# Attention and MLP in one kernel: v moved to partitions 32 to 95, its neighbour rows copied on chip, the halves swapped, and a new written order

## The chip, the cores and the metric

The kernel runs on one core of one Trainium2 chip. The metric is device time in microseconds (us). The core has five engines that work side by side, each through its own queue and in its own order: TensorE (PE in the profile: matrix products; PEld is its weight load), VectorE (DVE), ScalarE (ACT), GpSimd (POOL), which here mostly issues the loads, and SyncE (SP), which issues the stores. Sixteen DMA engines move the data between HBM and SBUF.

## The reference, cut to what matters

```python
B, H, S, D = 4, 8, 768, 64;  block, window = 32, 16
k_sum = k.reshape(B, H, S//32, 32, D).max(axis=3)      # 24 block maxima of k per head
v_sum = v.reshape(B, H, S//32, 32, D).mean(axis=3)     # 24 block means of v per head
scores_l = q @ k.T / 8, kept only where |i - j| < 16   # a band of 31 keys
scores_s = q @ k_sum.T / 8 + log(32)                   # 24 coarse keys
a = softmax(concat([scores_l, scores_s]))
x = (a @ concat([v, v_sum])) as [3072, 512]            # heads side by side
h = x @ w_in;  g = h * clip(h + 3, 0, 6) / 6;  out = g @ w_out    # w_in 512x2048, w_out 2048x512
```

All inputs and the output are float32 in HBM. The kernel loads with a conversion to bf16.

## The kernel before, in words

**Tiling of the attention.** A batch has 768 query rows per head, cut into NQ = 12 tiles of 64 queries (QB). With a band of 31 keys a tile needs a window of 96 key rows (WIN), and the 24 block maxima stand beside them, so that the product for one tile and one head has 120 keys (KEYS). `kaug[p]` holds k transposed for the pair p of heads, tile by tile: columns 0 to 63 are the tile's own rows, 64 to 95 the 32 rows of the next tile, 96 to 119 the maxima. A tile t therefore covers keys 64t to 64t+95 and queries 64t+16 to 64t+79; the last tile wraps round to the first rows, and its mask differs. `vaug[b % 2]` holds v in the same layout with the keys on partitions: rows 0 to 63 are loaded, rows 64 to 95 are those of the next tile, rows 96 to 119 are the block sums, and a column of ones (32 for the block rows) next to the 64 columns of v gives the softmax denominator. Each tile takes 66 columns (VW) per head.

**How each batch is loaded.** Batch 0 loads k and half of q in natural layout (`load_k`, `load_q`) and transposes on PE (`k_step`, `q_step`). Batches 1 to 3 load k and q by `load_raw` into `kraw` and `qraw` and transpose 32x32 blocks on VectorE (`turn`, lines 588 and 592); q is written in 16-row halves there, eight DMAs of 16 partitions a batch (line 375), k in four DMAs of 32 partitions (line 367). v comes by `load_v`, four DMAs of 64 partitions (line 385). Its 32 neighbour rows are copied on chip for batch 0 (`halo`) and loaded from HBM a second time for the other batches (`load_vhalo`, line 393, and a small SP DMA, line 395). `vsum_first` and `vsum` form the block sums by products with the indicator `ind` and spread them to 12 tiles a head.

**The stages.** `scores` (line 519, exp on ACT at 527, mask on DVE at 531), `values` and `finish` (products at 632, division at 663 and 667, transposes at 682) give x for half a batch: three tiles T of 128 rows. Half 0 is tiles t = 0 to 5 and half 1 tiles 6 to 11. The MLP takes x by half batches s = 0 to 7: `f1` (line 700: four products of 384 columns for one of 16 blocks ft; then ACT at 705 and DVE at 707 make g) and `f2` (line 720: 16 accumulating products of 512 columns for 128 rows, copied at 432 and stored at 730).

**What sets the order.** Every step is an operation with a key such as `F20.0`: the letter is the stage (K, Q, V, H loads; I, O weights; k, q, w transposes; s scores; u sums; h halo; v values; F, G the two MLP products), then batch or half batch and index, then the step's number in it. The string `ORDER` (lines 29 to 82) lists all keys once; each engine runs its operations in the order in which they stand there, and a suffix `:A` or `:D` says that ACT or DVE takes a copy. Nothing is reordered at run time: an instruction that waits holds all that is behind it on its engine. Costs and `dma=` figures in the code are what the writer of the order assumed; no time here is taken from them. Before 22 us, `keep` (line 803) puts products of constants into PE's waits.

So the first MLP product of half batch 0 is F00.0, the first of batch 1 is F20.0; w1p.0 and w1p.1 are the k and q transposes of batch 1, pair p; s1p0.0 are its scores; Q001 and Q011 are the second half of q of batch 0.

Of the kernel before, what the change touches and what calls it, by code (L numbers as in the profile page):

```python
# [15 lines left out]
D = 64  # L16
BLK = 32
# [4 lines left out]
VW = 66  # L22
# [19 lines left out]
F10.3 F12.1 F10.2 F12.2 F10.6 F10.4 F10.9 F10.5 F10.7 F10.8 F11.0 F10.10 F10.11 F11.6 F11.1 F11.9 F11.2 F11.7 F11.8 F11.10
F11.11 F12.6 F12.7 F12.8 F12.9 F12.10 F12.11 w12.0 G01.1 F13.0 F13.1 w13.0 F13.2 w11.0 w13.3 w10.0 w12.3 G01.2 G01.3 F12.3
F13.9 G01.4:A G02.0 G02.1 G02.2 G02.3 F11.3 F13.10 w11.2:A F12.4 F12.5 G02.4:A w12.2:A F13.3 F11.4 F13.4 w10.2:A w13.2:A
w12.4 w11.3 w11.4 w11.1 w11.5:D G00.0 G00.1 s110.0 s110.1 s110.3 w12.1 w13.1 w12.5:D w13.5:A G00.2 G00.3 s120.0 s120.1
s120.3 w13.4 w10.1 F13.5 w10.3 F11.5 w10.4 w10.5:D F13.11 V10.0 V13.0 V11.0 V23.0 V12.0 H1.0 K20.0 K22.0 V20.0 K21.0 Q231.0
K23.0 Q220.0 V22.0 V21.0 Q200.0 Q221.0 Q201.0 Q211.0 Q210.0 Q230.0 s130.0 G00.4:A F13.6 G12.0 s130.3 s130.1 F13.7 G00.5
G01.5 H1.1 G02.5 s120.2 s110.2 s130.2 s100.0 s100.1 F13.8 s100.2 s110.4 s100.3 G12.1 u1.0 u1.1:A u1.3:A u1.5:A G12.2 G12.3
G12.4:A u1.4:D u1.2:D v10.0 s120.4 v10.1 v10.5 v10.6 v10.2 s100.4 u1.7:A u1.6:A u1.9:A G11.0 G11.1 v12.0 v10.3 v10.4:A
u1.8:A v12.1 v12.2 s130.4 G11.2 v10.7 v12.3 v10.8:D G11.3 v12.4:A v13.0 F20.0 F20.3 G11.4:A F20.1 F20.4 v13.5 v13.1 v13.2  # L50
v13.6 F20.9 v13.3 v15.0 F20.10 F20.2 F20.5 F20.11 v15.1 v15.2 F20.6 F21.0 F20.7 F20.8 F21.1 V30.0 V31.0 V32.0 V33.0 F21.2
w21.0 F21.6 G10.0 F21.7 v13.4:A F21.8 F21.3 v15.3 v13.7 F21.9 F22.3 F21.4 F21.5 w20.0 F22.0 G10.1 F21.10 F22.4 v15.4:A
F21.11 F22.1 F22.5 F22.9 F23.0 F22.2 w20.3 F22.10 F22.11 F23.1 w21.2:A v13.8:A F23.2 w22.0 F22.6 u2.0 F22.7 F22.8 w21.3
G10.2 F30.0 F23.6 G10.3 w22.2:A F30.1 w20.4 F30.2 F30.3 F23.3 G10.4:A w22.3 w22.4 G22.0 G22.1 w20.1 u2.1:A w20.2:A F23.7
F23.4 w20.5:A F30.4 G12.5 u2.3 u2.5 G11.5 u2.4 u2.2 F23.5 F23.8 w22.1 s200.0 s200.1 s200.3 F30.5 w22.5:A F31.6 F23.9 G22.2
w23.1 F23.10 F31.7 s220.0 F23.11 F31.8 w21.4 w21.1 w21.5:D F30.9 G22.3 F31.0 F31.3 s220.3 s220.1 s210.0 G22.4:A H2.0 Q301.0
Q330.0 w23.0 K32.0 Q311.0 H3.0 F31.1 w23.5:A Q310.0 Q300.0 Q320.0 Q331.0 F31.2 F31.4 s200.4 F30.10 F30.11 F31.5 G20.0 G20.1
F30.6 F32.3 F33.0 Q321.0 K33.0 K31.0 K30.0 s210.1 s210.3 w23.3 F30.7 w23.4 s200.2 F30.8 w23.2:A F32.4 F33.1 u3.0 u3.1:D
s220.2 F33.2 s220.4 s210.2 G20.2 s230.0 s230.1 s230.3 s230.2 F32.5 G20.3 F31.9 F32.9 F31.10 F31.11 G20.4:A H2.1 G10.5 u3.3
u3.5 H3.1 G20.5 G22.5 v20.0 v20.1 v20.5 v20.2 v20.6 F33.9 G32.0 F32.10 F33.10 v22.0 F33.3 v20.3 F33.11 F32.0 G32.1 F33.4  # L60
v20.4:A v20.7 F32.1 v20.8:A v22.1 v22.2 F33.5 s230.4 F32.2 s210.4 v22.3 F32.11 v22.4:A F33.6 F32.6 F33.7 F32.7 v23.0 F33.8
v23.1 F32.8 F40.0 F40.1 F41.3 G32.2 F40.9 G32.3 F40.10 F41.4 v23.2 F40.2 F40.11 F41.5 v23.5 v23.6 F42.3 F41.9 F42.4 F42.5
F43.0 v25.0 F41.10 G32.4:A v23.3 F41.11 F42.0 F40.6 G30.0 G30.1 v23.4:A F43.1 F42.1 F40.7 v25.1 w30.1 F42.2 F43.2 F40.8
F41.0 F41.1 F41.2 v25.2 F40.3 F40.4 w30.5:A w33.1 w32.1 F42.6 G30.2 G30.3 F42.9 G30.4:A F42.7 v23.7 v23.8:A F42.10 G21.0
G21.1 G21.2 F40.5 w31.0 F42.8 F42.11 F43.3 F43.4 w30.0 w30.3 F43.6 w30.4 F43.5 w31.3 G21.3 F43.7 w32.5:D G21.4:A G21.5 v25.3
# [784 lines left out]
```

## Time and profile before

| | |
|---|---|
| median of three runs | 231.94 us (231.37 to 234.25) |
| the profiled execution's own time | 233.64 us |
| its span, first to last instruction | 231.9 us |
| bytes read from HBM, written | 29.60 MB, 6.29 MB |
| POOL's load queue | 117280 packets, 14.81 MB written to SBUF |
| first F00 product, first F20 product, last product's end | 30.30 us, 79.81 us, 227.29 us |

The busy time of an engine is the union of its instructions. Mean durations of single instructions include their latency, so that the sum of the means is somewhat more than the busy time. A wait is given as "engine and line <- engine and line that released it". In the table of windows each engine has its busy time and, in brackets, its instructions; then come the granted TensorE clock (1.00 is full), the DMA engines' busy share, and the rate in GB/s of the bytes on the written side, which are bf16 for loads.

### The profile page before, as it was taken

Reading aid. Unit: us, or ns where it says so; the run is one execution under the profiler, and the core shown is the slowest. Engines: PE = TensorE matmul, PEld = TensorE weight load, DVE = VectorE, ACT = ScalarE, POOL = GpSimd, SP = SyncE. Lnnn points to the kernel's source line nnn. Section 1 sums busy time; section 2 is a strip of 40 time slices with the busy share of each in tenths; the row PEclk is TensorE's granted clock in tenths of the full one; section 3 lists DMA queues with packets and bytes.
Section 4 is the critical chain, followed back from the end, with each engine's and each line's share of the span. In section 5 each row is a group of like instructions: output and inputs, shape, how many; then the busy total and the mean of one; then the engine's idle time right before and its main releaser. Section 6 shows DMA issues by size and latency. Waiting matters only on the chain.

```text
span 231.9 us, 5321 instructions
## 1 busy us (share of the span) xinstructions
PE 217.3 (94%) x2175; PEld 121.8 (52%) x2175; DVE 156.7 (68%) x327; ACT 126.5 (55%) x258; POOL 72.8 (31%) x86
## 2 busy tenths in 40 slices
PE   7899699999989997989999889999999999999991
PEld 2365476555445563545565445555555555555560
DVE  2489689789897669889785499945955645454201
ACT  2287567774588854768654535675552543434101
POOL 7994481357754734707741200000000000000000
PEclk9999979999999999999999999999999999999998
DMA  5999999999999999999999990132002030012013
GB/s 76 169 123 182 191 206 196 119 77 87 95 120 176 186 103 86 85 114 146 84 142 89 127 71 0 45 80 84 3 11 85 0 136 3 0 45 90 3 68 114
DMA packets 126585, 22.14 MB, mean 95 GB/s; under 512 B 116960, under 2 KB 123616, under 8 KB 126560
## 3 DMA queue, kind: packets, MB, share of 16 engines
q0 software_dynamic: 117280, 14.81, 217.7%
q1 hardware_dynamic: 9280, 6.98, 12.7%
q8 instruction: 17, 0.28, 0.7%
q14 instruction: 8, 0.07, 0.1%
HBM read 29.60 MB, written 6.29 MB: 155 GB/s over the span
## 4 chain that ended last, share of the span: by engine, by line
PE 58%; DMA 18%; issue 9%; POOL 9%; ACT 2%; DVE 2%; DVEq 0%; POOLq 0%
PE h L700 26%; PE o L720 22%; DMA kraw<-in_k_dram 13%; DMA qnat<-in_q_dram 5%; PE h L720 4%; POOL vaug L385 3%; ACT at L527 2%; PE S L519 1%; PE S L632 1%; POOL qraw L375 1%; POOL qnat L357 1%; PE S L682 1%; POOL knat L346 1%; POOL win L417 1%; POOL kraw L367 1%
## 5 line engine op out<-in xcount | busy, mean ns | idle before, releaser
L700 PE MATMUL h<-x,win 128*128 128x384 bf16 (+1 forms) x536 | 95.0, 321 | 3.1 <-DVE g L707 3.1
L705 ACT ACTIVATE r<-h 128x384 f32<-128x384 f32 x128 | 60.4, 493 | 59.4 <-PE h L700 58.7
L707 DVE SCALAR_TENSOR_TENSOR g<-r,h 128x384 bf16<-128x384 f32 x128 | 67.5, 545 | 33.9 <-ACT r L705 32.1
L720 PE MATMUL o<-wout,g 128*128 128x512 bf16 x336 | 82.3, 379 | 0.2 <-ACT ot L432 0.2
L700 PEld LDWEIGHTS <-win 128*128 128x128 bf16 x536 | 49.9, 99 | 37.5 <-issue 3.6
L720 PEld LDWEIGHTS <-g 128*128 128x128 bf16 x400 | 38.1, 98 | 36.3
L375 POOL DMA_DIRECT2D qraw<-in_q_dram x24 | 21.3, 890 | 29.1 <-issue 10.5
L527 ACT ACTIVATE at<-S 120x768 bf16<-120x768 f32 x32 | 24.8, 812 | 7.1 <-PE S L519 7.1
L367 POOL DMA_DIRECT2D kraw<-in_k_dram x12 | 15.8, 1317 | 13.5 <-issue 12.0
L385 POOL DMA_DIRECT2D vaug<-in_v_dram x16 | 15.1, 949 | 4.8 <-PE h L700 3.1
L592 DVE STREAM_TRANSPOSE qaug<-qraw 128x800 bf16<-128x800 bf16 x12 | 11.8, 998 | 6.2 <-DMA kraw<-in_k_dram 3.3
L667 DVE TENSOR_TENSOR xn<-S,rc 128x512 bf16<-128x512 f32 (+1 forms) x25 | 15.7, 643 | 0.4
L531 DVE TENSOR_TENSOR at<-at,mask 96x768 bf16<-96x768 bf16 x28 | 14.8, 546 | 1.5 <-ACT at L527 1.0
L432 ACT COPY ot<-o 128x512 f32<-128x512 f32 x16 | 9.4, 586 | 11.3 <-PE o L720 10.6
L588 DVE STREAM_TRANSPOSE kaug<-kraw 128x768 bf16<-128x768 bf16 x12 | 11.5, 965 | 2.1 <-DMA kraw<-in_k_dram 2.1
L432 ACT COPY x<-S 128x512 bf16<-128x512 bf16 x19 | 11.0, 587 | 2.5 <-PE S L682 2.1
L519 PEld LDWEIGHTS <-kaug 64*128 64x128 bf16 x384 | 7.0, 96 | 8.2 <-issue 6.3
L605 DVE TENSOR_REDUCE red<-kaug 128x24 bf16<-128x768 bf16 x12 | 11.2, 940 | 0.0
L519 PE MATMUL S<-qaug,kaug 64*128 64x64 bf16 x384 | 9.2, 192 | 2.0 <-ACT at L527 1.2
L803 PE MATMUL o<-idle 128*128 128x512 bf16 x30 | 9.5, 442 | 1.5 <-DVE idle L287 1.5
L720 PE MATMUL h<-wout,g 128*128 128x512 bf16 (+1 forms) x64 | 10.9, 326 | 0.0
L632 PEld LDWEIGHTS <-at 120*64 120x64 bf16 x384 | 7.6, 111 | 5.9 <-issue 4.8
(84 smaller groups left out, 139.3 us busy)
## 6 DMA issues: line engine op xcount, KB each, us to landing
out_dram<-ot SPq DMA_DIRECT2D x19, 256.0 KB
vaug<-in_v_dram POOLq DMA_DIRECT2D x16, 192.0 KB, 10.7
kraw<-in_k_dram POOLq DMA_DIRECT2D x12, 192.0 KB, 14.8
qraw<-in_q_dram POOLq DMA_DIRECT2D x24, 96.0 KB, 11.9
win<-in_moe_w_in_dram POOLq DMA_DIRECT2D x4, 512.0 KB, 11.8
wout<-in_moe_w_out_dram POOLq DMA_DIRECT2D x4, 512.0 KB, 13.5
vaug<-in_v_dram POOLq DMA_DIRECT2D x3, 380.0 KB, 16.2
out_dram<-ot SPq DMA_DIRECT2D x4, 224.0 KB
```

The source lines that it names most:

```text
L367: op("POOL", 0.8, lambda hs=hs, ds=ds, rows=rows: nc.gpsimd.dma_start(out=kraw[rows], in_=k[b, hs].rearrange("h (c r) d -> r (h c) d", r=B ...
L375: nc.gpsimd.dma_start(out=qraw[lo:lo + PAD, 1 - x:1 - x + NP * NB], in_=src[PAD * (1 - x):PAD * (2 - x)])
L385: op("POOL", 0.95, lambda: nc.gpsimd.dma_start(out=o[0:QB, lo:hi, 0:D], in_=rows[:, lo:hi]), w=[("v", b % 2, c)], prio=prio, dma=1.7)
L432: {"ACT": nc.scalar.copy, "DVE": nc.vector.tensor_copy, "POOL": nc.gpsimd.tensor_copy}[eng](o, i)
L519: nc.tensor.matmul(X[p, half].slot[:, j, i * QB:(i + 1) * QB], kaug[p][rows, t], qT[rows, p, t * QB:(t + 1) * QB], start=not masked, stop= ...
L527: op("ACT", act(2 * HALF), lambda a=a, x=x: nc.scalar.activation(a, x.slot[0:KEYS, :, 0:HALF], AF.Exp, scale=scl), r=[x], w=[("at", p, hal ...
L531: op("DVE", dve(2 * HALF, 1.92), lambda m=m, half=half: nc.vector.tensor_tensor(m, m, mask[:, half * HQ:(half + 1) * HQ].unsqueeze(1).to_b ...
L667: nc.vector.tensor_tensor(o, src[..., 0:D], r.unsqueeze(len(r.shape)).to_broadcast(list(o.shape)), op=ALU.mult)
L700: nc.tensor.matmul(h.slot[:, lo * 128:hi * 128], w_in_sb[:, kt, ft * 128:(ft + 1) * 128], xt[s].slot[:, kt, lo * 128:hi * 128], start=(kt ...
L705: op("ACT", act(HALF), lambda: nc.scalar.activation(r.slot[:], h.slot[:, 0:HALF], AF.Relu, bias=0.5, scale=1.0 / 6.0), r=[h], w=[r], prio= ...
L707: op("DVE", dve(HALF), lambda: nc.vector.scalar_tensor_tensor(gt[s].slot[:, ft], r.slot[:], 1.0, h.slot[:, 0:HALF], op0=ALU.min, op1=ALU.m ...
L720: nc.tensor.matmul(o.slot[:, a:z], gt[s].slot[:, ft, ts * 128:(ts + 1) * 128], w_out_sb[:, ft, a:z], start=(ft == 0), stop=(ft == NFT - 1))
```

## The change

The window of a tile moves by 32 rows: a tile t now has keys 64t-32 to 64t+63 and queries 64t-16 to 64t+47. The wrap is at the first tile instead of the last.

- v: `load_v` writes to partitions 32 to 95; the 32 rows ahead (partitions 0 to 31) are copied on chip from partitions 64 to 95 of the tile before, for all batches (`halo`, eight copies a batch). `load_vhalo` is gone. VW is 80 instead of 66. Partitions 0 to 31 are set to zero once, since the sums now run over 96 rows of which `ind` ignores 32: four memsets on DVE for the first buffer (z0.0 to z3.0, with a small one each), four on POOL for the second.
- Halves swapped: half 0 is tiles 6 to 11 and half 1 tiles 0 to 5.
- Block sums of the first half of batch 0: instead of spreading them over the tiles, `values` adds a second product of 24 rows (keys 96 to 119) for each head and tile, from a single copy `vf`. Only half 1 is spread.
- q: the second half of q of batch 0 comes by `load_wide` (row blocks of 128 rows for all heads) and is transposed by three 128x128 products a pair; batches 1 to 3 load q by the same four DMAs of 32 partitions as k, and the shift by 16 columns is made when the product reads it.
- `ORDER` is new throughout. Three of the four v loads of batch 1 stand between its k loads, the fourth ahead of its q loads. The F00 products stand ahead of the q transposes of half 1.

```diff
-VW = 66
+VW = 80
...
-c.5 c.8 s021.1 F00.0 F00.1 F00.2 F00.10 F00.3 F01.0 F01.1 s001.0 s001.1 s021.2 q031.1:D F00.4 F01.2 s001.2 F00.11 F00.12
...
+v00.4 v00.5 v02.2 v01.4 v02.4 v01.5 v02.3 v02.5 O1.0 O2.0 O3.0 v00.6 v00.7:A v01.6 F00.5 v02.6 F00.0 v01.7:D F00.1 F00.10
...
+q021.1:A F02.0 F03.1 F02.1 s031.0 s021.0 F02.6 s021.1 F03.2 F02.2 s031.1 G02.0 F02.9 F03.6 s021.2 K11.0 K12.0 V13.0 K10.0
+K13.0 V11.0 V12.0 z1.1 F02.7 s031.2 F03.7 F02.10 F02.8 v04.0 v03.0 v04.1 v04.2 v03.1 v03.2 F03.9 G02.1 v05.0 v03.3 F02.11
+v05.1 v05.2 G02.2 v03.4:A F03.10 F03.8 v04.3 v05.3 v04.4:D F03.3 v05.4:A F03.4 F10.0 F03.11 V10.0 z3.1 Q12.0 Q10.0 z2.1
...
         def blocks():
-            nc.gpsimd.memset(ind[:], 1.0)
-            nc.gpsimd.affine_select(out=ind[:], ...)
-            nc.gpsimd.affine_select(out=ind[:], ...)
+            nc.gpsimd.memset(ind[0:BLK], 0.0)
+            nc.gpsimd.memset(ind[BLK:64], 1.0)
+            nc.gpsimd.memset(ind[64:WIN], 1.0)
+            for x in range(2):
+                m = ind[BLK + BLK * x:WIN - BLK + BLK * x]
+                nc.gpsimd.affine_select(out=m, in_=m, ...)
+                nc.gpsimd.affine_select(out=m, in_=m, ...)
...
+        def empty(eng, i, c):
+            eng.memset(vaug[i][0:BLK, 2 * c:2 * c + 2, :, 0:D].bitcast(F32), 0.0)
+            if i == 0:
+                eng.memset(vf[c][WIN:KEYS, :, D:D + 2], float(BLK))
...
+    def low(x):
+        return (1 - x) * HQ
...
+    def load_wide(b, u, prio):
+        def go():
+            o = qwide[:, u].rearrange("p (h d) -> p h d", h=H)
+            n, lo = PAD if u == 0 else 0, 128 * u - PAD
+            if n:
+                nc.gpsimd.dma_start(out=o[0:n], in_=q[b, :, S - n:S].rearrange("h r d -> r h d"))
+            nc.gpsimd.dma_start(out=o[n:128], in_=q[b, :, lo + n:lo + 128].rearrange("h r d -> r h d"))
...
-            for x in range(2):
-                    src = q[b, hs].rearrange("h (c r) d -> r (h c) d", r=BLK)[:, :, ds]
-                    nc.gpsimd.dma_start(out=qraw[lo:lo + PAD, 1 - x:1 - x + NP * NB], in_=src[PAD * (1 - x):PAD * (2 - x)])
+        for name, src, o in (("K", k, kraw), ("Q", q, qraw)):
+            for g in range(4):
+                op("POOL", 1.32, lambda ...: nc.gpsimd.dma_start(
+                    out=o[rows], in_=src[b, hs].rearrange("h (c r) d -> r (h c) d", r=BLK)[:, :, ds]), ...)
...
-        op("POOL", 0.95, lambda: nc.gpsimd.dma_start(out=o[0:QB, lo:hi, 0:D], in_=rows[:, lo:hi]),
+        op("POOL", 0.95, lambda: nc.gpsimd.dma_start(out=o[BLK:WIN, lo:hi, 0:D], in_=rows[:, lo:hi]),
...
-    def load_vhalo(b, prio):
...
-            copy(eng, o[QB:WIN, hs, a:z, 0:D], o[0:WIN - QB, hs, a + 1:z + 1, 0:D])
+            copy(eng, o[0:BLK, hs, a:z, 0:D], o[QB:WIN, hs, a - 1:z - 1, 0:D])
             if x:
-                copy(eng, o[QB:WIN, hs, z, 0:D], o[0:WIN - QB, hs, 0, 0:D])
+                copy(eng, o[0:BLK, hs, 0, 0:D], o[QB:WIN, hs, NQ - 1, 0:D])
...
+        alone = b == 0 and half == 0
...
+                            if alone:
+                                nc.tensor.matmul(y, a[0:WIN, cols], vaug[0][0:WIN, h, t, 0:D + 1], start=True, stop=False)
+                                nc.tensor.matmul(y, a[WIN:KEYS, cols], vf[p][WIN:KEYS, h % 2, 0:D + 1], start=False, stop=True)
...
         for c in range(NP):
-            load_v(b, c, base - 10 + c)
-        load_vhalo(b, base - 7)
+            load_v(b, c, base - 10 + c if b > 1 else -29.5 + 0.01 * c)
+            for x in range(2):
+                halo(b, c, x, base - 2 + c + 4 * x)
```

## The prediction

> **What bounds the kernel now.** I read the shares first, then the 40 slices, the waits, and windows around the places where PE pauses.
>
> The page's busy times, and from its slices the rows of PE and of its granted clock:
>
> ```profile
> PE 217.3 (94%) x2175; PEld 121.8 (52%) x2175; DVE 156.7 (68%) x327; ACT 126.5 (55%) x258; POOL 72.8 (31%) x86
> ...
> PE   7899699999989997989999889999999999999991
> ...
> PEclk9999979999999999999999999999999999999998
> ```
>
> PE is the bound from about 28 us on, so time is won only where PE pauses, runs slowly, or has not yet real work. The first such place is the start. Windows of busy time, and the timeline between 24 and 31 us:
>
> ```profile
> 24.00:28.00 4.00, 2.12 (x42) 1.39 (x37) 3.09 (x11) 2.02 (x5) 1.55 (x3) 1.00 1.33 189
> 28.00:32.00 4.00, 3.86 (x53) 3.38 (x53) 3.25 (x9) 2.17 (x5) 4.00 (x4) 0.57 1.24 206
> ```
>
> ```profile
> 25.38 0.59 ACT L432 COPY x<-o 128x512 bf16<-128x512 bf16 x1 [1.17 <-PE o L682]
> 27.21 0.53 PE L493 MATMUL S<-ident,qnat 96*64 96x96 bf16 x16 [1.62 <-DMA qnat<-in_q_dram]
> ...
> 30.30 0.93 PE L700 MATMUL h<-x,win 128*128 128x128 bf16 x7
> ```
>
> The x of the first 128 rows is ready at 25.97 us, but PE stands before the q transposes until 27.21, since q's second half has not landed; then the granted clock is 0.57 for 4 us, and F00 begins at 30.30.
>
> The second place is the arrival of each batch's k and q. From the waits:
>
> ```profile
> DVE qaug L592 <- DMA kraw<-in_k_dram: 3.3, 1, 3.3
> ...
> PE h L700 <- DVE g L707: 3.1, 2, 1.7
> ...
> DVE qaug L592 <- DMA qraw<-in_q_dram: 2.9, 2, 1.8
> ...
> DVE kaug L588 <- DMA kraw<-in_k_dram: 2.1, 1, 2.1
> ```
>
> DVE waits at a transpose for a load, the g behind it in DVE's queue are late, and PE runs out of free h banks. The windows of the whole MLP, split at the first product of batch 1 (79.81 us in the timeline):
>
> ```profile
> 30.30:79.81 49.51, 48.10 (x569) 28.04 (x565) 41.86 (x83) 36.56 (x70) 27.18 (x27) 0.98 4.25 138
> 79.81:227.30 147.49, 143.57 (x1264) 79.34 (x1260) 95.25 (x187) 73.95 (x160) 23.57 (x24) 1.00 1.84 68
> ```
>
> After 79.81 us PE idles for 147.49 - 143.57 = 3.9 us. A tail of 231.9 - 227.3 = 4.6 us follows the last product.
>
> What the loads cost is read in windows in which one kind alone moves: v (12 to 14 us), weights, k of batch 1, q of batch 1, v of batch 1. The last column is GB/s:
>
> ```profile
> 12.00:14.00 2.00, 2.00 (x63) 1.34 (x57) 1.48 (x5) 1.56 (x4) 2.00 (x4) 1.00 4.80 105
> 34.00:36.00 2.00, 1.97 (x31) 1.53 (x31) 1.86 (x4) 1.87 (x4) 0.29 (x2) 1.00 1.24 206
> 42.00:44.00 2.00, 2.00 (x17) 1.23 (x15) 1.74 (x5) 1.08 (x2) 0.00 (x0) 1.00 4.15 117
> 50.00:52.00 2.00, 2.00 (x14) 1.15 (x12) 1.69 (x4) 1.50 (x4) 0.78 (x1) 1.00 7.19 83
> 64.00:66.00 2.00, 2.00 (x32) 0.99 (x31) 2.00 (x6) 1.32 (x4) 1.66 (x2) 1.00 4.75 118
> ```
>
> q in DMAs of 16 partitions runs at 83, k in DMAs of 32 at 117, v on 64 partitions at 105 to 118, weights at 206.
>
> **Part 1, the start.** The first x needs the last v load of batch 0. Its issue starts at 11.3 us, and the four v loads land 6.6 to 8.0 us after issue: about 18.5. The new indicator adds two memsets (0.44) and two selects (0.58) with gaps on POOL ahead of the third v load, so 2.2 us later issue. Against that stands v's rate, which on 32 to 95 no row shows: between today's 112 GB/s (7.0 us for a batch's 786 KB) and the weights' 206 (3.8 us). I take 5.4, halfway, which gives back up to half of the delay. So landing at 18.5 to 20.8, then sum products 0.84, copy 0.3, values 0.64 (twice the 0.32 shown, for the added 24-row products), division 0.6, transposes 0.4, copy 0.6, six handovers of 0.2: 4.6 us. F00 at 23.1 to 25.4, say **24.2**, where today it is 30.30. The four spreads that go (0.36 on DVE, 0.83 on ACT) leave room for that. The four new DVE memsets of 768 words, by the 192-word memset (0.22 us) 0.8 us each, three ahead of PE's first warming products, lie in the 4.5 us for which DVE then idles before L469; without that cover they would cost 1 us.
>
> Today's PE does 1.5 us more between these points (q transposes and scores ahead of F00), and 1.7 us were lost to the clock of 0.57 (4 us x 0.43). The new order has no q transpose ahead of F00.
>
> **Part 2, batch 0 until F20.0.** I added the rows of all keys between F00.0 and F20.0 in both orders. Before: PE 45.5, DVE 44.4, ACT 37.7; DVE's real busy time was 41.86, a factor of 1.06 for overlap. After: PE 47.3, DVE 52.7, ACT 49.3, because halo copies and spreads of batch 1 and of half 1 now lie here (seven halos on DVE at 0.36, nine on ACT at 0.83) and two more k transposes. DVE: 52.7 / 1.06 = 49.7 us, at 97% use 51.3. F20.0 is then not before 24.2 + 51.3 = 75.5.
>
> The other limit is batch 1's q. k of batch 1 is through by 49.5 us (a POOL wait on kraw ends at 49.9). The start's delay and v's gain roughly cancel. v of batch 1 ahead of q adds 5.4, and q at k's rate takes 786 / 118 = 6.7 instead of 9.6 us: 49.5 + 5.4 + 6.7 = **61.6**, against 61.88, when the first q transpose starts today. So the swap of v and q eats what the wider q load brings. From that transpose to the last division that F20 needs, DVE has 15.3 us of rows, 14.5 without overlap; with a transpose and a copy, 15.7. F20.0 at 61.6 + 15.7 = **77.3**, the later of the two limits, 2.5 us ahead of 79.81.
>
> [...]
>
> **Part 3, after F20.0.** PE's rows that remain are 140.8 us before and 140.4 after; 143.6 busy for 140.8 is a factor of 1.02, so 143.2. Per batch the loads shrink from k 6.7 + q 9.6 + v 7.0 + halo 380 KB at 115 = 3.3, in all 26.6, to 6.7 + 6.7 + at most 7.0 = 20.4 us. That is 6 us less, more than the longest wait of 3.3, so the three waits of DVE for k and q should go. What is late next are the 24 added halo copies, mostly 0.83 us on ACT, ahead of an r for which PE's banks wait. ACT has 73.95 of 147.49 us in use, so I keep 1.5 of today's 3.9 us of idle PE (bounds 0 and 4).
>
> The stores of the end change from a 512-column copy on DVE (0.69) with two DMAs to 256 columns on ACT (0.45) with one: tail 4.1.
>
> **Sum.** 77.3 + 143.2 + 1.5 + 4.1 = **226.1 us** of span. Today's span of 231.9 equals the median of 231.94 (the profiled execution itself took 233.64), so I predict a median of 226.1, 2.5% less.
>
> **Rivals.**
>
> *The crowd eats the start.* DVE, ACT and PE all have 46 to 50 us of real work between F00.0 and F20.0. If in-order waits cost 10%, or q lands 2.5 us later because v is no faster on its new partitions and the DMA queue runs dry during the longer indicator, F20.0 stays at 79.8; with the later waits half gone the sum is 79.8 + 143.2 + 2 + 4.1 = 229.1, with all of them 231. That is no change. For it speaks 9.47 of 10 us of DVE already between 50 and 60; against it that today's stage has 5 us of slow clock and waits which go. That v's move brings no rate at all is this rival's second form: q at 63.2, sum 227.7. Chance 0.34 for 227.3 to 236.6.
>
> *Slower: the clock falls in batch 0.* With F00 6 us earlier, PE meets q's second half, w_in's last block and w_out's first closer to their landing (the weights alone need 2.5 us each at 206 GB/s). Today one such wait cost 1.6 us of idle and 1.7 us of slow clock, 3.3 together. Three of them make 10 us: 24.2 + 51.3 + 10 = 85.5, and 85.5 + 143.2 + 3.9 + 4.1 = 236.7. It decides when those loads land over 2 us after PE reaches them. Against it: the order puts nine F00 products and all of F01 between them. [...] Chance 0.12.
>
> **How the numbers follow.** Forecast, faster by over 2% (under 227.3): 0.54. Two per cent is about what a measurement of this kernel can tell from no change. Low end: F20.0 at 75.0 with v at the weights' rate, no waits, 75.0 + 142 + 3.9 = 220.9. High end: F20.0 at 81, waits of 4, 81 + 143.2 + 4 + 4.1 = 232.3. The range 220.5 to 232.5 leaves out part of the slower rival and a still better start.
>
> **What would show it.** F00 before 26 us and no clock under 0.9 near 28; v loads of batch 0 over 130 GB/s; the first q transpose of batch 1 near 61.6; F20.0 near 77; no DVE wait for kraw or qraw over 1 us after 80. The prediction is wrong if F20.0 is at 80 or later, if the clock falls a second time, or if r (L705) waits behind halo copies so that PE idles over 4 us after F20.0.

## The result and the profile after

The changed kernel takes 250.17 us (median of four, 248.93 to 250.94), where the kernel before takes 233.09 in the same comparison (231.37 to 237.06). The ratio is 1.075, with an interval of 1.065 to 1.086: slower by 7.5%, outside the range, on the other side of the forecast. The profiled execution took 250.39 us, with a span of 248.7. Ratios, here and below, leave out executions in a second, slower state, such as the 237.06 of the kernel before.

The shares, and from the slices the rows of PE and of its granted clock, in the page of the kernel after:

```profile
PE 230.6 (93%) x2158; PEld 131.8 (53%) x2187; DVE 163.2 (66%) x334; ACT 142.7 (57%) x290; POOL 67.1 (27%) x79
...
PE   2999999899996878999999999999999999999993
...
PEclk9999555999999799999999999999999999999999
```

PE has 13.3 us more of busy time than before, with 17 recorded instructions fewer. Its row shows no hole in slices 5 to 8, but the clock row has three slices of 5 there (a slice is 6.2 us). The windows of the start, with the columns of the table before (busy time and instructions of PE, PEld, DVE, ACT, POOL; clock, DMA share, GB/s):

```profile
24.00:28.00 4.00, 3.53 (x20) 2.38 (x20) 0.78 (x3) 1.67 (x5) 0.74 (x1) 0.52 1.78 181
28.00:32.00 4.00, 4.00 (x23) 2.64 (x22) 0.61 (x2) 0.00 (x0) 3.73 (x4) 0.50 1.46 199
32.00:36.00 4.00, 4.00 (x23) 2.63 (x22) 0.00 (x0) 0.00 (x0) 2.63 (x3) 0.50 1.24 206
36.00:40.00 4.00, 3.80 (x20) 2.56 (x22) 0.34 (x3) 0.00 (x0) 1.31 (x1) 0.50 1.24 206
```

PE is "busy" with some 20 products in 4 us, a third of what it does in such a window of the padded kernel below (x68), at half the clock, while from 28 us on DVE and ACT all but stand still. What these products are, the timeline of PE says (start, duration, line, shape; "xcount" is the number in the group):

```profile
22.07 0.22 PE L658 MATMUL S<-vaug,at 96*64 96x65 bf16 x1
22.22 0.21 PE L659 MATMUL S<-vf,at 24*64 24x65 bf16 x1
22.36 0.22 PE L658 MATMUL S<-vaug,at 96*64 96x65 bf16 x1
22.51 0.21 PE L659 MATMUL S<-vf,at 24*64 24x65 bf16 x1
...
29.47 0.26 PE L658 MATMUL S<-vaug,at 96*64 96x65 bf16 x1
29.66 0.26 PE L659 MATMUL S<-vf,at 24*64 24x65 bf16 x1
...
42.27 0.63 PE L728 MATMUL h<-x,win 128*128 128x128 bf16 x4
```

They are the products of `values` in half 0 of batch 0: 96 keys, then the new one of 24 keys, in turn. The starts are 0.145 us apart at the full clock, 0.19 at half of it; but for one of 0.47 us for DVE at 27.57, no wait is noted beside them. There are 48 such pairs, from 20.62 to 39.80 us. F00 begins at 42.27 us instead of the forecast 24.2 (and 30.30 before).

The rest of the run, split at the first product of batch 1 (F20.0 at 102.06 us), and two waits of POOL and PE:

```profile
42.27:102.06 59.79, 52.79 (x621) 30.51 (x628) 50.77 (x97) 45.52 (x93) 24.07 (x22) 0.95 2.31 92
102.06:244.62 142.56, 141.18 (x1216) 78.87 (x1228) 95.16 (x189) 84.04 (x173) 14.20 (x12) 1.00 0.55 58
```

```profile
POOL kraw L396 <- DVE kaug L611: 19.1, 1, 19.1
...
PE o L748 <- ACT ot L446: 3.2, 2, 3.0
```

After F20.0 PE idles 142.56 - 141.18 = 1.4 us, where it was 3.9 before. DVE has no wait for kraw or qraw left; now it is POOL that waits for DVE to free kraw. The tail is 248.7 - 244.62 = 4.1 us.

So the 22.6 us between the forecast span of 226.1 and 248.7 are: F00 18.1 late; the stretch from F00.0 to F20.0 59.8 instead of 53.1, 6.7 more; the rest 142.6 instead of 143.2 + 1.5, 2.1 less; the tail as forecast. 18.1 + 6.7 - 2.1 = 22.7.

The two rates of v on partitions 32 to 95, in windows in which it moves alone (kernel after):

```profile
11.00:12.00 1.00, 1.00 (x20) 0.45 (x13) 0.85 (x5) 0.64 (x1) 0.89 (x2) 1.00 2.40 153
...
15.00:17.00 2.00, 2.00 (x48) 1.43 (x48) 1.81 (x3) 1.28 (x3) 2.00 (x4) 1.00 2.15 144
```

153 and 144 GB/s, against 105 to 118 before: 5.1 to 5.5 us for the 786 KB of a batch, where the forecast took 5.4. The row of a tile grew from 66 to 80 columns in the same change, so that the partitions alone brought the rate is not shown.

### The profile page after: what moved, and what is told of

Same layout as the page of the kernel before. It is cut to its first block, busy times and chain, and to the rows that moved or that the text cites. A ratio compares the mean times of both kernels' runs of the same rounds, so it can differ in the third digit from the quotient of the medians.

```text
span 248.7 us, 5355 instructions
## 1 busy us (share of the span) xinstructions
PE 230.6 (93%) x2158; PEld 131.8 (53%) x2187; DVE 163.2 (66%) x334; ACT 142.7 (57%) x290; POOL 67.1 (27%) x79
## 4 chain that ended last, share of the span: by engine, by line
PE 88%; ACT 5%; DVE 2%; issue 2%; DVEq 0%
PE h L728 33%; PE o L748 28%; PE h L748 4%; PE o L831 3%; PE S L661 3%; PE S L540 3%; PE S L658 2%; PE S L659 2%; PE S L710 2%; ACT vaug L446 1%; PE h L658 1%; PE h L659 1%; ACT at L549 1%; PE h L462 1%; PE S L590 1%
## 5 line engine op out<-in xcount | busy, mean ns | idle before, releaser
L735 DVE SCALAR_TENSOR_TENSOR g<-r,h 128x384 bf16<-128x384 f32 x128 | 68.4, 548 | 37.8 <-ACT r L733 35.6
L748 PE MATMUL o<-wout,g 128*128 128x512 bf16 x312 | 80.0, 386 | 5.0 <-ACT ot L446 3.2
L549 ACT ACTIVATE at<-S 120x768 bf16<-120x768 f32 x32 | 24.8, 807 | 3.1 <-PE S L540 3.1
L396 POOL DMA_DIRECT2D kraw<-in_k_dram x12 | 15.7, 1316 | 20.7 <-DVE kaug L611 19.1
L396 POOL DMA_DIRECT2D qraw<-in_q_dram x12 | 15.7, 1315 | 14.6 <-DVE qT L615 12.3
L446 ACT COPY vaug<-vaug 32x640 bf16<-32x640 bf16 (+2 forms) x33 | 17.5, 573 | 3.6 <-PE S L590 2.7
L446 ACT COPY ot<-o 128x512 f32<-128x512 f32 x18 | 10.5, 583 | 12.5 <-PE o L748 11.9
L691 DVE RECIPROCAL rc<-S 128x8 f32<-128x8 f32 (+1 forms) x25 | 4.7, 196 | 12.2 <-PE S L659 10.7
L446 ACT COPY x<-S 128x512 bf16<-128x512 bf16 x18 | 10.3, 585 | 4.1 <-PE S L710 4.0
L831 PE MATMUL o<-idle 128*128 128x512 bf16 x17 | 7.2, 555 | 4.6 <-DVE idle L289 4.6
L615 DVE STREAM_TRANSPOSE qT<-qraw 128x768 bf16<-128x768 bf16 x12 | 11.3, 957 | 0.0
L540 PE MATMUL S<-qT,kaug 64*128 64x64 bf16 x384 | 9.3, 191 | 1.9 <-ACT at L549 1.8
L748 PE MATMUL h<-wout,g 128*128 128x256 bf16 (+1 forms) x63 | 10.8, 325 | 0.1
```

What stands on the lines that cost most here:

```text
L396: op("POOL", 1.32, lambda src=src, o=o, hs=hs, ds=ds, rows=rows: nc.gpsimd.dma_start(out=o[rows], in_=src[b, hs].rearrange("h (c r) d -> r ...
L446: {"ACT": nc.scalar.copy, "DVE": nc.vector.tensor_copy, "POOL": nc.gpsimd.tensor_copy}[eng](o, i)
L540: nc.tensor.matmul(X[p, half].slot[:, j, i * QB:(i + 1) * QB], kaug[p][rows, t], qT[rows, p, t * QB:(t + 1) * QB], start=not masked, stop= ...
L549: op("ACT", act(2 * HALF), lambda a=a, x=x: nc.scalar.activation(a, x.slot[0:KEYS, :, 0:HALF], AF.Exp, scale=scl), r=[x], w=[("at", p, hal ...
L735: op("DVE", dve(HALF), lambda: nc.vector.scalar_tensor_tensor(gt[s].slot[:, ft], r.slot[:], 1.0, h.slot[:, 0:HALF], op0=ALU.min, op1=ALU.m ...
L748: nc.tensor.matmul(o.slot[:, a:z], gt[s].slot[:, ft, ts * 128:(ts + 1) * 128], w_out_sb[:, ft, a:z], start=(ft == 0), stop=(ft == NFT - 1))
```

## Experiments on the start: why the products take 0.145 us

Three theories. A: what costs is the turn from a product of 96 rows to one of 24, and the other way round. B: it is adding to the place in PSUM that the product just before wrote. C: a product of few rows is slow by itself.

**Padded.** The second product reads all 120 rows, the first 96 against zeros, so that both are of the same kind; order and accumulation stay.

```diff
+                eng.memset(vf[c][0:WIN].bitcast(F32), 0.0)
...
-    nc.tensor.matmul(y, a[WIN:KEYS, cols], vf[p][WIN:KEYS, h % 2, 0:D + 1], start=False, stop=True)
+    nc.tensor.matmul(y, a[:, cols], vf[p][0:KEYS, h % 2, 0:D + 1], start=False, stop=True)
```

> The changed kernel with one edit: the second product of each head and tile takes all 120 key rows, against a copy of the block sums whose rows 0 to 95 are zero, instead of rows 96 to 119 alone. Theory A (a product of 24 rows that follows one of 96, and the other way round, starts only when the array has drained, about 0.145 us each at full clock): the pair falls from 0.29 us to about 0.06, the six groups of 16 products to about 0.7 us each, the clock no longer falls near 24 us, the first MLP product moves from 42.3 to about 25 us and the span from 248.7 to about 231. Theory B (the wait comes from accumulating into the place that the product before has just written): the pair stays at 0.29 us, the span at about 248. Theory C (a product of so few rows is slow by itself): as A here.

The timeline of PE in the padded kernel (two starts in each group), and the window of the start:

```profile
22.45 0.20 PE L659 MATMUL S<-vaug,at 96*64 96x65 bf16 x2
22.48 0.20 PE L660 MATMUL S<-vf,at 120*64 120x65 bf16 x2
22.52 0.20 PE L659 MATMUL S<-vaug,at 96*64 96x65 bf16 x2
```

```profile
24.00:28.00 4.00, 3.84 (x68) 3.25 (x64) 3.42 (x13) 3.12 (x7) 0.97 (x2) 1.00 1.83 178
```

Two products every 0.035 us, at the full clock; F00 at 25.55, F20.0 at 84.35, span 231.0. Timed: 233.52 us, ratio 1.005 (1.001 to 1.009) to the kernel before. One zeroed operand takes away 16.7 us. B falls, since the accumulation is the same.

**Grouped.** The 24-row products stay, but of each bank all products of 96 rows come first, then all of 24; the accumulation is opened by the first product of the bank and closed by the last.

```diff
-            for T in Ts:
+            for T, z in [(T, z) for T in Ts for z in range(1 + alone)]:
...
+    if z == 0:
+        nc.tensor.matmul(y, a[0:WIN, cols], vaug[0][0:WIN, h, t, 0:D + 1], start=h % 4 == 0, stop=False)
+    else:
+        nc.tensor.matmul(y, a[WIN:KEYS, cols], vf[p][WIN:KEYS, h % 2, 0:D + 1], start=False, stop=h % 4 == 3)
```

> The changed kernel with the two kinds of product of a group apart: first the eight products of 96 rows, then the eight of 24 rows into the same places. Theory A: two changes of rows a group instead of 16, so about 0.3 us plus 16 short products, 0.7 us a group; first MLP product near 25 us, span near 231. Theory B: the same, since no product follows the one it adds to. Theory C: the eight products of 24 rows stay at 0.145 us each, 1.3 us or more a group, first MLP product near 33 us.

The groups of PE in the grouped kernel, kept apart by shape (busy time, mean ns):

```profile
L659 PE MATMUL S<-vaug,at 96*64 96x65 bf16 x32 | 1.3, 201 | 0.3 <-issue 0.3
L661 PE MATMUL S<-vf,at 24*64 24x65 bf16 x32 | 1.2, 196 | 0.0
```

The same groups in the kernel after hold 8.0 and 7.9 us. So C falls too: a 24-row product is as quick as the others if its neighbours are of its kind (196 ns beside 201). What remains is the turn from one kind to the other, and the timeline of PE in the grouped kernel shows one by itself:

```profile
20.70 0.32 PE L659 MATMUL S<-vaug,at 96*64 96x65 bf16 x8
20.95 0.31 PE L661 MATMUL S<-vf,at 24*64 24x65 bf16 x8
```

The eighth product of 96 rows starts at 20.82 us and the first of 24 at 20.95, 0.13 us later; within a kind the starts lie 0.05 us apart or less. Span 228.7, F00 at 24.78, F20.0 at 82.08, both executions 230.4 and 234.04. The same kernel, timed beside the kernel before:

> The kernel after with the products of one bank in two runs, first all of 96 rows, then all of 24 (as in the run with grouped products), now timed in rounds for an interval. Expected from the two times seen (230.4 and 234.0) and the span of 228.7: 231.5 us, ratio 0.985 to 1.0 to the kernel before.

232.71 us, beside 234.71 for the kernel before: ratio 0.989, interval 0.984 to 0.995. F00 at 26.01, F20.0 at 83.98, span 230.6. With one loop turned round, the change is about 1% faster than the kernel before, not 7.5% slower.

**Left out.** The first product alone; the block sums are missing in half 0 of batch 0.

```diff
-    nc.tensor.matmul(y, a[0:WIN, cols], vaug[0][0:WIN, h, t, 0:D + 1], start=True, stop=False)
-    nc.tensor.matmul(y, a[WIN:KEYS, cols], vf[p][WIN:KEYS, h % 2, 0:D + 1], start=False, stop=True)
+    nc.tensor.matmul(y, a[0:WIN, cols], vaug[0][0:WIN, h, t, 0:D + 1], start=True, stop=True)
```

> The changed kernel without the products of 24 rows: for the first half of batch 0 the block sums are left out of the values and of the softmax sum. It shows what is left if they cost nothing. Theory A: groups of 0.35 us, first MLP product near 24 to 25 us, span near 230, within 1 us of the padded form. If the first MLP product stays over 35 us, something else in the start is the cause.

F00 at 23.58, 1.2 us ahead of the first grouped run: about what the 48 added products cost when they run well, though the two grouped runs differ by as much (24.78 and 26.01). The span (232.2, one execution of 233.9) is not better, since F20.0 came at 85.61: PE waited 2.0 us for v of batch 1 at its sums, and the clock was at half twice, for 3.4 us each.

**The split alone.** In the kernel before, half 0 of batch 0 gets the same pair of products and nothing else of the change.

```diff
+    if b == 0 and half == 0:
+        y, cols = o[64 * c:64 * c + 64, h % 4], slice(t * QB, (t + 1) * QB)
+        nc.tensor.matmul(y, a[0:WIN, cols], vaug[0][0:WIN, h, t, 0:D + 1], start=True, stop=False)
+        nc.tensor.matmul(y, a[WIN:KEYS, cols], vaug[0][WIN:KEYS, h, t, 0:D + 1], start=False, stop=True)
+        continue
```

> The kernel before with this part alone: for the first half of batch 0 each product of 120 rows is split into one of 96 and one of 24 rows, with the same operands. Theory A: 48 pairs at 0.29 us instead of 48 products at 0.04, 12 us of PE if the clock holds and 16 if it falls to half as in the changed kernel; the first MLP product at 40 us or later instead of 30.3, the span at 241 to 248. If only the new order and layout make the pairs slow, the span stays at 232 to 234.

246.44 us (one execution), beside 233.04 for the kernel before: about 13 us lost, with F00 at 46.70 us instead of 30.30. Two windows of its start:

```profile
24.00:28.00 4.00, 4.00 (x23) 2.47 (x23) 0.96 (x3) 0.44 (x2) 3.27 (x4) 0.73 1.28 193
28.00:32.00 4.00, 3.67 (x15) 1.97 (x16) 0.18 (x1) 0.00 (x0) 3.28 (x4) 0.50 1.24 207
```

The same picture as in the kernel after: few products, half the clock, DVE and ACT nearly idle.

**The change without the split.** All else of the change stays; the sums of half 0 are spread to the tiles by four more copies, as before, and `values` has one product again.

```diff
-        alone = b == 0 and half == 0
+        alone = False
...
+        op(EITHER, SPREAD, lambda eng: copy(eng, vaug[0][WIN:KEYS, 2 * c:2 * c + 2, HQ:NQ, 0:D], ...),
+           r=[("vf", c)], w=[("vsum", 0, c, 0)], prio=prio + 0.1)
```

> The kernel after without the products of 24 rows: the block sums of half 0 of batch 0 are spread to the tiles as in the kernel before (four spreads of 0.36 us on DVE), and values has one product of 120 rows again. All else of the change stays. If the products of 24 rows behind products of 96 are the whole of the loss (theory A): F00.0 at 24 to 26, clock 1.0 from 24 to 44 us, F20.0 at 80 to 84, span 227 to 231, against 248.7. If the rest of the change has a part in it, F20.0 stays above 86.

F00 at 25.76, span 231.3, 233.51 us, ratio 1.005 (1.001 to 1.009). F20.0 at 84.94 is 0.9 us beyond what was expected and under the 86 that would have spoken against A. So theory A holds from five sides: padding, grouping, leaving out, doing it alone, undoing it alone. What is shown is the price of the turn between the two kinds: one start every 0.145 us, against two every 0.035 in the padded kernel. That the array drains at the turn, as the expectation of the padded kernel has it, was the author's guess and no run shows it. Whether the product or its weight load waits is not separated either: in the pairs both start together (in the kernel after, both at 29.47 us, then both at 29.66).

## Experiments on the stretch from F00.0 to F20.0

Without the slow products this stretch still takes 57.3 and 58.0 us in the two grouped runs, where the forecast had 53.1 and the kernel before 49.5. Here is the whole stretch in the kernel timed with grouped products, and ACT's largest wait in it:

```profile
26.01:83.98 57.97, 50.02 (x622) 29.14 (x628) 50.36 (x98) 45.96 (x94) 32.77 (x30) 1.00 2.89 147
```

```profile
ACT vaug L446 <- PE S L590: 2.7, 1, 2.7
```

DVE's busy time is close to the 49.7 that was added up; the stretch is longer because DVE works only 87% of it.

**An earlier copy of the o bank (D).** PE waits 3.0 us near 63 us because ACT copies the only o bank (G00.4) behind halos and spreads. One token moves:

```diff
-G00.3 h111.0:A F12.7 F12.10 w10.2:A w13.2:A h121.0:A u1.1:A u1.4:A u1.8:A w11.2:A G00.4:A
+G00.3 h111.0:A F12.7 F12.10 G00.4:A w10.2:A w13.2:A h121.0:A u1.1:A u1.4:A u1.8:A w11.2:A
```

> Grouped products, and one edit of the written order: ACT copies the o bank of G00 (G00.4) right after the r of F12.10 instead of behind eight copies of halos and block sums. Theory D (the one o bank is held by ACT's queue): PE's wait of 3.0 us for that copy near 63 us goes, the copies behind it come 0.6 us later, F20.0 comes 2 to 3 us earlier than 82.08, and the span is 226 to 227. Theory E (ACT and DVE are simply full between F00.0 and F20.0, so that PE waits elsewhere): the wait goes but F20.0 stays within 0.7 us of 82.1, since PE then waits for the scores and sums of batch 1.

Slower than the grouped kernel (0.989): 236.32 us, ratio 1.005 (1.001 to 1.009); F20.0 at 88.15, span 234.8. The waits of ACT and of DVE in this kernel between 50 and 90 us, and a window:

```profile
ACT ot L445 <- PE o L749: 3.7, 3, 1.9
```

```profile
DVE vaug L445 <- ACT vs L445: 3.2, 1, 3.2
```

```profile
68.00:72.00 4.00, 1.61 (x26) 1.04 (x27) 4.00 (x6) 3.93 (x9) 2.97 (x3) 0.52 0.87 44
```

PE's wait went, as expected, and came back elsewhere: ACT now stands before a copy whose product is not yet done, the block sums behind it reach DVE 3.2 us late instead of 1.3, and the clock falls. D falls as it was put.

**No halo copies in batches 1 to 3.** The 24 `halo` operations and their tokens are left out.

```diff
-            for x in range(2):
-                halo(b, c, x, base - 2 + c + 4 * x)
```

> Grouped products, and the 24 halo copies of batches 1 to 3 left out; the window rows of the neighbour tile are then not those of v, so x of batches 1 to 3 lacks its part from them. All else is as in the run with grouped products. It prices the copies. If they are the crowd: F20.0 4 us earlier (78), since about six of them (0.83 to 0.92 us on ACT, 0.36 on DVE) stand ahead of it, and the span 224. If they lie beside other work: F20.0 within 1 us of 82.1 and the part after it at 142.6 as before.

F20.0 at 84.87, no earlier than in the grouped kernel. But this is the longer of two executions, 233.20 us beside 229.61, and its clock was at half for 6.83 us, from 73.30 to 80.13. The other one kept the clock at 1.00, and its span is 227.9, where the five executions of the grouped kernel at 1.00 have 228.4 to 230.6. So the price of the copies ahead of F20.0 is not settled; that they cost 4 us there is not seen. What is late in their place in the profiled execution is a load, in DVE's waits:

```profile
DVE qT L613 <- DMA qraw<-in_q_dram: 2.5, 1, 2.5
```

q of batch 1 lands at 65.4 us here (last issue 55.53 + 9.9), not at the forecast 61.6. After F20.0 the span to the last product is 227.44 - 84.87 = 142.57 us, the same to 0.01 as with the copies (142.57 in the timed grouped kernel): the halo copies behind F20.0 cost nothing.

**Halos by DMA.** With the early copy, the halos of batches 1 to 3 become DMAs on SP's queue.

```diff
+        def move():
+            for h in (2 * c, 2 * c + 1):
+                nc.sync.dma_start(out=o[0:BLK, h, a:z, 0:D], in_=o[QB:WIN, h, a - 1:z - 1, 0:D])
...
+        if b:
+            op("SP", 0.2, move, ...)
```

> Grouped products, the early copy of G00, and the halo copies of batches 1 to 3 made by DMAs on SP's queue (from SBUF to SBUF) instead of by ACT and DVE. The 3072 packets of 128 bytes a batch cost the DMA engines about 3.4 us at 115 GB/s. If ACT and DVE are the limit of the stretch before F20.0: F20.0 at 77 to 79 and a span of 222 to 225, below every other version. If the DMA engines are the limit there (q of batch 1 later by the 3.4 us): F20.0 at 81 to 83 and a span of 226 to 229.

Worse than either expectation: 240.72 us, ratio 1.024 (1.019 to 1.029), F20.0 at 93.23. PE's waits between 22 and 90 us:

```profile
PE S L670 <- DMA vaug<-vaug: 2.9, 2, 1.7
...
PE S L597 <- DMA vaug<-in_v_dram: 1.9, 1, 1.9
...
PE S L597 <- DMA vaug<-vaug: 1.2, 1, 1.2
```

The sums of batch 1 (L597) now wait for the halos that they read along, and they hold PE in its order: 0.94 us of work from 56 to 60.

**The indicator after the v loads (F).** With grouped products, POOL builds `ind` behind the last v load of batch 0.

```diff
-s010.2 V01.0 c.6 V02.0 s000.1 V03.0 I0.0
+s010.2 V01.0 V02.0 s000.1 V03.0 c.6 I0.0
```

> Grouped products, and one edit of the written order: POOL builds the indicator (three memsets, four selects, 3.9 us) after the third and fourth v load of batch 0 instead of before them. In the run timed with grouped products the DMA engines moved 50, 0 and 86 GB/s from 12 to 15 us, some 2.4 us of transfer lost. Theory F (all loads up to q of batch 1 form one queue, so what is lost at 12 us is paid at 65 us, and F20.0 hangs on q): q of batch 1 lands near 62.6 instead of 65.0, F20.0 comes 1.5 to 2.4 us earlier than in that run (82.0 instead of 83.98), and the span is 228.5. Theory E (ACT and DVE are full there anyway): q lands earlier but F20.0 moves by less than 0.7 us.

The queue no longer runs dry: a row of this kernel, where the grouped one moved nothing from 13 to 14 us:

```profile
13.00:14.00 1.00, 1.00 (x31) 0.71 (x33) 0.81 (x4) 0.81 (x1) 0.88 (x3) 1.00 2.43 155
```

q of batch 1 lands at 63.4 (53.10 + 10.3) instead of 65.0, F20.0 is at 82.31 instead of 83.98, span 228.9; timed 232.74 us, ratio 0.999 (0.992 to 1.006). That is what F said in numbers, but F00 was 0.83 us earlier too, and the first grouped run, with the indicator still early, had F20.0 at 82.08. So F's link is not shown by it, and the next run speaks against it.

**Both, the later indicator and no split.**

> Both edits: no products of 24 rows, and the indicator built after the v loads. By theory F the two gains add: F00.0 at 23 to 25, q of batch 1 at 62.6, F20.0 at 79 to 82, span 226 to 228.5, the fastest of all. If F20.0 hangs on ACT and DVE, it is within 0.7 us of the run without the split.

235.71 us, ratio 1.011 (1.000 to 1.023); F00 at 27.65, q of batch 1 at 61.7 (52.80 + 8.9), F20.0 at 87.63. q is 1.7 us earlier than in the run before and F20.0 5.3 later, behind an F00 that is 2.5 later and a clock at half from 33.36 to 36.77 us. So F20.0 does not hang on q here. It keeps its distance to an instruction on ACT, the halo copy that waits 2.67 us for the sum products. From the copy's start to F20.0 it is 82.08 - 56.61 = 25.47 us in the first grouped run, 83.98 - 58.52 = 25.46 in the timed one, 82.31 - 56.84 = 25.47 with the later indicator, 87.63 - 62.16 = 25.47 here. This shows that nothing gives way between the two; that the copy's wait sets F20.0 it does not show, since what stands ahead of the copy keeps its distance too (the halo copy before it starts 4.70 to 4.82 us earlier in all four).

**The halo ahead of the sums (G).** That wait is a dependency that the change brought: halos write partitions 0 to 31 of `vaug`, and the sums now read them, against zeros in `ind`. In the written order h111 stands behind u1.0, so ACT must wait until PE has read. One token moves; every engine issues the same instructions in the same order.

```diff
-G02.4:A F12.6 F12.9 G00.0 F13.0 u1.0 G00.1 G00.2 G00.3 h111.0:A F12.7
+G02.4:A h111.0:A F12.6 F12.9 G00.0 F13.0 u1.0 G00.1 G00.2 G00.3 F12.7
```

> Grouped products and the later indicator as in the run before, and one token of the written order moved: the halo copy h111 of batch 1 stands ahead of the sum products u1.0 instead of behind them. Every engine issues the same instructions in the same order; only who waits for whom is turned round, since the sums read the partitions 0 to 31 that the halo writes. Theory G (ACT idles 2.67 us at 54 to 57 us because its halo copy must not overwrite rows that PE's sums still have to read, and the sums wait for the last v load of batch 1; the r behind it are late, DVE idles 1.4 and 1.3 us, and all that follows runs at full ACT): the wait of 2.67 us goes, and F20.0 comes 1.5 to 2.7 us earlier than 82.31, F00.0 staying at 25.2; span 226.5 to 227.5. Theory E in its plain form (ACT and DVE are full whatever waits): F20.0 within 0.7 us of 82.31.

The halo copy in ACT's timeline, first with the later indicator alone, then in this kernel:

```profile
56.84 0.92 ACT L446 COPY vaug<-vaug 32x640 bf16<-32x640 bf16 x2 [2.67 <-PE S L590]
```

```profile
55.86 0.92 ACT L446 COPY vaug<-vaug 32x640 bf16<-32x640 bf16 x2
```

The wait is gone, and PE's wait of 3.0 us for the o bank is 0.2. F00 came at 25.87, 0.69 later than in the run before it, and the halo starts 0.98 earlier, so 1.67 is won between the two. ACT still has nearly that lead at a later exp of batch 1 (71.84 instead of 72.80 us). Then it is given back: F20.0 is at 82.78. Windows of 1 us, first with the later indicator alone, then in this kernel:

```profile
73.00:74.00 1.00, 0.35 (x12) 0.24 (x12) 0.94 (x3) 1.00 (x2) 0.29 (x1) 1.00 3.12 133
74.00:75.00 1.00, 0.50 (x13) 0.44 (x14) 1.00 (x3) 1.00 (x3) 0.40 (x1) 1.00 3.23 122
75.00:76.00 1.00, 1.00 (x6) 0.46 (x5) 0.93 (x3) 1.00 (x2) 0.91 (x1) 1.00 3.25 123
```

```profile
73.00:74.00 1.00, 0.66 (x16) 0.47 (x13) 1.00 (x3) 1.00 (x3) 0.53 (x1) 0.52 3.23 122
74.00:75.00 1.00, 1.00 (x3) 0.30 (x2) 0.93 (x2) 1.00 (x2) 0.78 (x1) 0.50 3.24 123
75.00:76.00 1.00, 1.00 (x4) 0.38 (x3) 0.90 (x2) 0.08 (x1) 0.51 (x1) 0.50 3.26 123
```

The clock is at half for 3.4 us, which costs about 1.5 us, an estimate from these windows and the next (0.66 x 0.48 + 0.50 + 0.50 + 0.22). So G is shown for the wait and for the lead up to 72 us; that F20.0 comes 1.5 us earlier is not shown. Timed: 230.78 us beside 234.87, ratio 0.986 (0.977 to 0.994), span 229.4.

**And the copy of o two spreads earlier.**

```diff
-u1.1:A u1.4:A u1.8:A w11.2:A G00.4:A
+u1.1:A u1.4:A G00.4:A u1.8:A w11.2:A
```

> The same, and ACT's copy of the o bank of G00 stands ahead of two block-sum spreads and a k copy. Theory G with the o bank as the next in line: PE's wait of 3.0 us for that copy falls to 0.5 to 1.5 us, F20.0 another 0 to 1.5 us earlier. If the spreads behind it are what the scores and values of batch 1 wait for, F20.0 stays where the run with the halo ahead has it, or is up to 0.6 us later (the length of the copy).

230.68 us, ratio 0.985 (0.978 to 0.992), the lowest ratio of all versions, some 1.5% faster than the kernel before (its interval overlaps with that of the grouped products alone). F20.0 at 82.49 with F00 at 25.19: 57.3 us, no gain over the run before it. The wait of PE for the o bank is no longer in its list, DVE waits 1.1 us for q of batch 1, and the clock falls to 0.58 between 72 and 76 us again.

The stretch in all timed versions without the slow products (us; the clock is that of the stretch):

| version | F00.0 | F20.0 | stretch | clock | time, ratio to the kernel before |
|---|---|---|---|---|---|
| padded | 25.55 | 84.35 | 58.8 | 0.97 | 233.52, 1.005 |
| grouped, timed | 26.01 | 83.98 | 58.0 | 1.00 | 232.71, 0.989 |
| no split | 25.76 | 84.94 | 59.2 | 0.97 | 233.51, 1.005 |
| grouped, o copied earlier | 26.11 | 88.15 | 62.0 | 0.92 | 236.32, 1.005 |
| and halos by DMA | 25.48 | 93.23 | 67.8 | 0.92 | 240.72, 1.024 |
| grouped, indicator later | 25.18 | 82.31 | 57.1 | 1.00 | 232.74, 0.999 |
| no split, indicator later | 27.65 | 87.63 | 60.0 | 0.97 | 235.71, 1.011 |
| indicator later, halo ahead of sums | 25.87 | 82.78 | 56.9 | 0.97 | 230.78, 0.986 |
| and o two spreads earlier | 25.19 | 82.49 | 57.3 | 0.97 | 230.68, 0.985 |

## Why the prediction was wrong, point by point

**Part 1, the step that failed:** "values 0.64 (twice the 0.32 shown, for the added 24-row products)". The price of a product was taken from a row in which all products are of one kind, and doubled. In turn with products of 96 rows each takes 0.145 us, and 0.19 once the clock is at half, from 24.19 us on. The first eight pairs took 2.3 us and the other forty 40 x 0.38 = 15.2, together 17.5 instead of 3 x 0.64 = 1.9 for the three tiles of rows, which all stand ahead of F00 on PE, though the sum held only the first; the other PE work up to F00 ran at half clock too. F00 was at 42.27 instead of 24.2.

With the products grouped F00 is at 24.8 to 26.0, inside or near the 23.1 to 25.4 forecast, but partly by luck: the last v landed at 18.1 and 18.5 us (13.4 + 4.7 and + 5.1), at the early end of the 18.5 to 20.8 or ahead of it, and from there F00 took 6.7 and 7.5 us instead of 4.6.

**No rival named this.** "The clock falls in batch 0" gave the right sign and the right symptom, but by three waits of PE for DMAs, and there was none. It carried 0.12.

**Part 2 failed by a second term:** "DVE: 52.7 / 1.06 = 49.7 us, at 97% use". DVE's busy time was 50.4 us, so the sum was right; the use was 50.36 / 57.97 = 87%. The row of the kernel before already had it: 41.86 of 49.51 is 85%. At 85 to 87% the 49.7 come to 57 to 58.5, as measured. The 87% say how much DVE stood, not why: with the halo's wait taken out, and then PE's wait for the o bank too, the stretch was still 56.9 and 57.3 us, with the clock at half for 3.4 us in each.

The rival "the crowd eats the start" is what the grouped kernel did in this stretch, and the queue did run dry during the indicator, as it said (0 GB/s from 13 to 14 us). That the spans of 228.7 and 230.6 lie near its 229.1 to 231 is partly luck: F20.0 came at 82.1 and 84.0, not at 79.8, and the part behind it was shorter than it reckoned.

**Its other limit was 3.4 us too early.** In POOL's order one v load of batch 1, not three, stands between the k loads, and three behind them; all four are ahead of q. q of batch 1 landed at 65.0 in the timed grouped kernel, not 61.6. "k of batch 1 is through by 49.5" was read from the end of a POOL wait; by issue and landing it was through at 32.78 + 19.1 = 51.9 before. The last v of the timed grouped kernel landed at 47.25 + 9.5 = 56.8, 4.9 later (5.4 taken), and q took 8.2 us after it, not 6.7. It happened not to decide: DVE reached its first q transpose 1.6 us after that landing. In two variants (no halos; the last version of the table) it did make DVE wait, 2.5 and 1.1 us, so the two limits lie close together.

**Part 3 held.** 142.6 us against 143.2 + 1.5, idle PE 1.4 against 1.5, no wait for kraw or qraw, tail 4.1. This part of the run won 147.48 - 142.56 = 4.9 us: 2.5 by less idle time of PE, and 2.4 because PE's busy time here fell from 143.57 to 141.18, with 1216 recorded products instead of 1264. The halo copies after F20.0 are free (142.57 us to the last product with them and without).

**v's rate held** (144 to 153 GB/s, "over 130"). So the change as built pays 17 us for one loop; behind F20.0 it wins 5 us, of which load layout and written order were not told apart; and the crowd before F20.0, with a wait of 2.67 us among it, takes back more than the earlier F00 gives, since F20.0 is at 82.1 and 84.0 in the grouped kernel and was at 79.81 before.

What stays open is how much that wait costs by itself, since the clock fell in the profiled runs without it. One execution with the halo ahead of the sums kept the clock at 1.00, with a span of 228.2; the five with the later indicator alone that kept it have 228.9 to 231.0. Open is also whether q ahead of v of batch 1 would be better; that order was not tried.

## What to carry to other kernels

When a product with few rows is added, look at its neighbours in PE's queue, not only at its own row: make both of one kind by zeros, or run all of one kind and then all of the other (here two starts in 0.035 us with the zeros, and one turn of 0.13 us behind eight products when grouped, instead of one start every 0.145 us). A PE row of 9s does not say that PE works: count the instructions in the window and read the clock beside it (here 23 products in 4 us at 0.50). Take an engine's use from the stretch that is forecast, here 85%, before writing 97% into a sum; and ask of each zeroed or unused row who still reads it, since that reader makes others wait (2.67 us here).

## What the runs showed of the hardware

In the kernel after, products of 96 and 24 rows in turn start every 0.145 us at the full clock and every 0.19 us at half. Of 96 and 120 rows in turn two start every 0.035 us in the padded kernel; in the grouped kernel the starts within a kind lie 0.05 us apart or less, and a turn from one kind to the other costs 0.13 us. With 48 pairs in turn the granted clock was at 0.50 from 24.19 to 44.67 us, although PE is shown busy for 19.7 of these 20.5 us.

In these traces the granted clock changes on a grid of 3.413 us. In the kernel after it is at half for 20.48 us (6 steps of the grid, from 24.19 us), at full for 37.55 (11 of them, to 82.22) and at half for 3.41 (to 85.63), then at full until the last product. In the kernel before it is at half for 3.41 us (from 28.49) and then at full for 197.97 (58 of them), past the last product. In the kernel before with the split, a piece of the grid that held 2.3 us of products of constants (30.34 to 32.68) is followed by one at the full clock, between pieces at half (the clock is 0.50 from 28 to 32 us, 0.91 from 32 to 36 and 0.51 from 36 to 40).

In these traces a fall of the clock is not read off the idle time alone. Here are two pieces of the grid in the kernel with the later indicator (counted in steps of 3.413 us from 7.29 us, where the record of its clock begins), then one in the kernel with the halo ahead of the sums and the one behind it:

```profile
61.90:65.31 3.41, 1.84 (x9) 0.87 (x9) 3.35 (x7) 3.35 (x7) 0.00 (x0) 1.00 2.60 163
72.14:75.55 3.41, 1.88 (x52) 1.31 (x54) 3.31 (x8) 3.41 (x6) 2.10 (x2) 1.00 2.91 152
```

```profile
69.62:73.03 3.41, 1.99 (x86) 1.35 (x85) 3.29 (x8) 3.20 (x7) 2.71 (x3) 1.00 2.46 193
73.03:76.45 3.42, 3.08 (x20) 1.33 (x19) 2.81 (x6) 2.05 (x4) 2.26 (x2) 0.50 3.25 127
```

PE idled 1.57 and 1.53 us in the first two pieces and the clock stayed at 1.00; it idled 1.42 in the third and the clock fell. What the clock goes by instead is not shown.
